# Output projection of a decode attention kernel: weights loaded last, behind the last V tile, and the product in four column tiles

## The chip, the cores and the metric

The kernel runs on one core of one Trainium2 chip. The metric is the device time of one execution in microseconds (us), the median of several. A program on one core has no second die to compare with, so a run is called "slow" only when it is over 1.5% above the fastest run of the same kernel. Profiles show a span a little shorter than the time (1277.4 us for 1279.2 us), and all positions in time below are us from the start of the profiled span.

## The reference, cut to what matters

```python
# A: attention for one new token, batch 2, 16 query heads over 8 KV heads, 32768 cached keys, head size 256
q = (x @ wq) ...                                         # x: [2, 1, 448]
k = jnp.repeat(k_cache, 2, axis=1)                       # k_cache, v_cache: [2, 8, 32768, 256] bf16
v = jnp.repeat(v_cache, 2, axis=1)
p = softmax(einsum("bhqd,bhkd->bhqk", q, k) * Dh ** -0.5)
a = einsum("bhqk,bhkd->bhqd", p, v) ... @ wo             # wo: [4096, 448]
# B: a small dense layer with GELU, w1 [448, 1792], w2 [1792, 448]
g = sigmoid((x * gate_w).sum(-1))
out = g * a + (1 - g) * b                                # [2, 1, 448]
```

The two caches are 537 MB of the 547 MB that the kernel reads, and each byte is read once.

## The kernel before

There are 16 groups (batch, KV head) of 2 K tiles and 2 V tiles. A tile is 8.39 MB: 128 partitions of 64 KB. Three slots hold the tiles; the sync engine (SP) issues the loads in a fixed order and waits before each for the release of its slot. The vector engine transposes each K tile in place, the tensor engine forms scores, then softmax, then the sum weighted over V. I call the last V tiles V29, V30, V31, and the last K tile K31. The tensor engine's main part is a hardware loop; the programs of the other engines are written out in full.

```python
order = [("WQ", 0), ("W12", 0)]
for i in range(NTILES + LAG):                 # LAG = 2
    if i < NTILES: order.append(("K", i))
    if i >= LAG and i - LAG < LASTV: order.append(("V", i - LAG))
order += [("WO", 0), ("V", LASTV)]            # WO takes the slot of V29, V31 the slot of K31
# ... [cut]
PIECES = (64, 32, 16, 8, 8)                   # V31 comes in 5 loads
```

The sync engine works this list in order, so V31, although its own slot (K31's) is free long before, stands behind WO, which waits for V29's weighted sum.

The last group has a form of its own: V is the stationary operand, 256 pairs of weight load and a 2-column matmul for each tile. All other groups have P as stationary operand (24 columns), 64 matmuls of 512 columns in four column tiles; their partial sums are gathered on the vector engine by 8 masked adds, and folded by 2 small matmuls (called OT here).

```python
for r in range(R):                            # last group only
    if r in ends: E.wait(f"pV{ends[r]}", ("piece", ends[r]))
    # ... [cut]
    for j in range(2):
        matmul(ps_o[:, 2*j:2*j+2], kv[:, r, j:Dh:2], pt[:, r16, i, 2*w:2*w+2], ...)

def FIN(c0, c1, key):                         # output product: 32 chunks of 128 rows of WO
    for c in range(c0, c1):
        matmul(ps_a, attnT[:, kvh, j, hh, :], wo_v[:, h, j*Dm:(j+1)*Dm], start=(c == 0), stop=(c == NCH-1))
        # ps_a is 2 partitions x 448

# end of the tensor engine's program
PV(LASTV - 1)
E.wait_total("d_wo")
E.wait("dve", ("O", NG - 2)); E.wait("dve", "bp")
FIN(0, NCH - 4, "FINA")
PV(LASTV)
E.wait("dve", ("O", NG - 1))                  # attnT of the last group
FIN(NCH - 4, NCH, "FIN")
# vector engine: out_sb = ps_a * g + bpart    (2 x 448, called mix here)
# sync engine:   out <- out_sb                (one store)
```

Of the kernel before, what the change touches and what calls it, by code (L numbers as in the profile page):

```python
# [121 lines left out]
def bass_gated_mix__gqa_block_cached__dense_activation_gelu__decode_kernel(  # L122
# [32 lines left out]
    P = 128  # L155
# [22 lines left out]
    GS = NG - 1  # L178
    PIECES = (64, 32, 16, 8, 8)
# [10 lines left out]
    for nm in ("d_w12", "d_wo", "d_x", "d_gw", "d_b", "d_out"):  # L190
        sch.stream(nm, 16)

    with contextlib.ExitStack() as es:
# [12 lines left out]
        b2_bf = PT[0:Bn, 512:512 + Dm]  # L206
        gp_sb = sb("gp_sb", [Bn, Dm], dt.float32)
        b2o, bpart = gp_sb, gp_sb
# [4 lines left out]
        g_sb = sb("g_sb", [Bn, 1], dt.float32)  # L213
        omg = sb("omg", [Bn, 1], dt.float32)
# [6 lines left out]
        out_sb = pexp[0:Bn, 0:Dm]  # L221
# [20 lines left out]
        ps_b = ps_f[0:Bn, 0:Dm]  # L242
        ps_a = ps_f[0:Bn, 0:Dm]
# [21 lines left out]
        order += [("WO", 0), ("V", LASTV)]  # L265
# [71 lines left out]
        def prog_sp(E):  # L337
# [3 lines left out]
            for d in order:  # L341
                for pd in before_of[d]:
                    E.wait("pe", released(pd))
                kind, idx = d
                if kind == "WQ":
                    parts = [(wq_f, A_wq[0:KC * P, :].rearrange("(p k) n -> p (k n)", p=P), "d_wq0"),
                             (wq_r, A_wq[KC * P:Dm, :].rearrange("p (h n) -> (p h) n", h=2), "d_wq1")]
                    for i, (o, src, _) in enumerate(parts):
                        dma(lambda e, o=o, src=src: e.dma_start(o, src), "slot0", ("wq", i))
                elif kind == "W12":  # L350
                    parts = [(w1_f, B_w1[0:KC * P, :].rearrange("(p k) n -> p (k n)", p=P)),
                             (w1_r, B_w1[KC * P:Dm, :].rearrange("p (h n) -> (p h) n", h=2)),
                             (w2_f, B_w2.rearrange("(p f) n -> p (f n)", p=P))]
                    for i, (o, src) in enumerate(parts):
                        dma(lambda e, o=o, src=src: e.dma_start(o, src), "d_w12", ("w12", i))
                elif kind == "WO":
                    dma(lambda e: e.dma_start(wo_v, A_wo.rearrange("(h i j) n -> i h (j n)", i=P, j=2)), "d_wo", "wo")
                elif d == ("V", LASTV):
                    src, base, r0 = kv_src(A_v_cache, idx), slot_of[d] * SLOT, 0
                    for i, n in enumerate(PIECES):  # L360
                        c0, c1 = r0 * Dh, (r0 + n) * Dh
                        dma(lambda e, c0=c0, c1=c1: e.dma_start(ring[:, base + c0:base + c1], src[:, c0:c1]),
                            f"pV{i}", ("piece", i))
                        r0 += n
                else:
                    src = kv_src(A_k_cache if kind == "K" else A_v_cache, idx)
                    dma(lambda e, src=src, d=d: e.dma_start(cut(slot_of[d], 0, SLOT), src),
                        f"slot{slot_of[d]}", ("fill", d))
            E.wait("dve", "mix")
            dma(lambda e: e.dma_start(out[:, 0, :], out_sb), "d_out", "out")  # L370
            E.wait_total("d_out")

        def prog_pe(E):
# [34 lines left out]
            def do_HT():  # L408
                E.wait_total("d_w12")
                for fc in range(FC):  # L410
# [10 lines left out]
            def do_FB():  # L421
                E.wait("dve", "hT")
                for fc in range(FC):
                    E.ins(lambda e, fc=fc: e.matmul(ps_b, hT_bf[:, fc, :], w2_v[:, fc, :],
                                                  start=(fc == 0), stop=(fc == FC - 1)),
                          key=("FB" if fc == FC - 1 else None))
# [52 lines left out]
            def PV(v):  # L479
# [8 lines left out]
                if g < GS:  # L488
                    for r4 in range(0, CR, 4):
                        for w in range(4):  # L490
                            for j in range(4):
# [7 lines left out]
                                if w == 0:  # L499
# [5 lines left out]
                                E.ins(fn, key=(("PV", v) if (r4 == CR - 4 and w == 3 and j == 3) else None))  # L505
                    return
                ends = {}
                if v == LASTV:
                    r0 = 0
                    for i, n in enumerate(PIECES):  # L510
                        ends[r0] = i
                        r0 += n
                for r in range(R):
                    if r in ends:
                        E.wait(f"pV{ends[r]}", ("piece", ends[r]))
                    k, r16 = divmod(t * R + r, CR)
                    w, i = divmod(k, 2)
                    for j in range(2):
                        E.ins(lambda e, kv=kv, r=r, r16=r16, i=i, w=w, j=j, t=t: e.matmul(  # L519
                            ps_o[:, 2 * j:2 * j + 2], kv[:, r, j:Dh:2], pt[:, r16, i, 2 * w:2 * w + 2],  # L520
                            start=(t == 0 and r == 0 and j == 0), stop=(t == NT - 1 and r == R - 1),
                            skip_group_check=True),
                            key=(("PV", v) if (r == R - 1 and j == 1) else None))

            def FIN(c0, c1, key):
                for c in range(c0, c1):
                    h, j = c // 2, c % 2
                    kvh, hh = h // 2, h % 2
                    E.ins(lambda e, c=c, kvh=kvh, hh=hh, j=j, h=h: e.matmul(
                        ps_a, attnT[:, kvh, j, hh, :], wo_v[:, h, j * Dm:(j + 1) * Dm], start=(c == 0), stop=(c == NCH - 1)),  # L530
                        key=(key if c == c1 - 1 else None))

            do_QT()
            do_HT()
# [21 lines left out]
            E.wait_total("d_wo")  # L556
            E.wait("dve", ("O", NG - 2))
            E.wait("dve", "bp")
            FIN(0, NCH - 4, "FINA")
            PV(LASTV)  # L560
            E.wait("dve", ("O", NG - 1))
            FIN(NCH - 4, NCH, "FIN")

        def prog_act(E):
# [8 lines left out]
            for b in range(Bn):  # L573
                dma(lambda e, b=b: e.dma_start(b2_bf[b:b + 1, :], B_b2.rearrange("(o k) -> o k", o=1)), "d_b", ("b2", b))
# [3 lines left out]
            E.ins(lambda e: e.activation(omg[:, :], gs_sb[:, :], ACTF.Exp, scale=-1.0), key="ge")  # L578
# [32 lines left out]
            for g in range(NG):  # L611
                chain(g)
                if g + 1 < NG:
                    fill_A(g + 1)

        def prog_dve(E):
            E.ins(lambda e: e.memset(ps_o[:, :], 0.0), key="o0")
            E.wait("pool", "idf")
# [18 lines left out]
            E.ins(lambda e: e.tensor_scalar(gs_sb[:, :], omg[:, :], 1.0, None, op0=ALU.add), key="g1")  # L637
            E.wait("dve", "g1")
            E.ins(lambda e: e.reciprocal(g_sb[:, :], gs_sb[:, :]), key="g")
            E.wait("dve", "g")  # L640
            E.ins(lambda e: e.tensor_scalar(omg[:, :], g_sb[:, :], -1.0, 1.0, op0=ALU.mult, op1=ALU.add), key="omg")
            E.wait_total("d_b")
            E.wait("dve", "omg")
            E.ins(lambda e: e.tensor_scalar(b2o[:, :], b2_bf, omg[:, 0:1], None, op0=ALU.mult), key="b2o")
# [21 lines left out]
            def do_bp():  # L666
                E.wait("pe", "FB")
                E.wait("dve", "b2o")
                E.ins(lambda e: e.scalar_tensor_tensor(out=bpart[:, :], in0=ps_b, scalar=omg[:, 0:1], in1=b2o[:, :],
                                                       op0=ALU.mult, op1=ALU.add), key="bp")  # L670
# [26 lines left out]
            def do_end(g):  # L697
                b, kvh = grp(g)
                E.wait("pe", ("PV", g * NT + NT - 1))
                col = C_OT  # L700
                src = ps_m
                if g < GS:
                    if g >= 1:
                        E.wait("pe", ("OT", g - 1))
                    for c in range(8):
                        i, w = c // 4, c % 4
                        p = ps_o[:, 512 * w + 256 * i:512 * w + 256 * i + 256]
                        if c == 0:
                            E.wait("dve", "mask")
                            E.ins(lambda e, p=p: e.tensor_scalar(o_sb[:, :], p, mask[:, 0:1], None, op0=ALU.mult),  # L710
                                  key=("OS0", g))
                        else:
                            E.wait("dve", ("OS" + str(c - 1), g))
                            E.ins(lambda e, p=p, c=c: e.scalar_tensor_tensor(  # L714
                                out=o_sb[:, :], in0=p, scalar=mask[:, c:c + 1], in1=o_sb[:, :],
                                op0=ALU.mult, op1=ALU.add), key=(("OS" if c == 7 else "OS" + str(c)), g))
                    E.wait("pe", ("OT", g))
                else:
                    src, col = ps_o, 0
                E.wait("dve", ("RL", g))  # L720
                for j in range(2):
                    E.ins(lambda e, j=j: e.tensor_tensor(attnT[:, kvh, j, :, b], src[:, col + 2 * j:col + 2 * j + 2],  # L722
                                                         rl[g % 2][:, :], ALU.mult),
                          key=(("O", g) if j == 1 else ("O0", g)))
# [13 lines left out]
            E.ins(lambda e: e.scalar_tensor_tensor(out=out_sb, in0=ps_a, scalar=g_sb[:, 0:1], in1=bpart[:, :],  # L738
# [49 lines left out]
```

## Time and profile before

| | before |
|---|---|
| time, median (range) | 1279.25 us (1279.17 to 1279.28) |
| span of the profiled run | 1277.4 us |
| bytes read, mean rate | 547.43 MB, 429 GB/s |
| busy share PE, DVE | 57%, 54% |
| last landing of a load | 1272.19 us |
| from there to the end of the span | 5.2 us |

First some lines of the profile page of the kernel before: its span; in 40 equal slices of the span the busy share of the DMA engines in tenths, and what they moved in GB/s; and of the table of DMA queues (packets, MB, share of 16 engines) the two queues that fetch instructions.

```profile
span 1277.4 us, 8610 instructions
...
DMA  9999999999999999999999999999999999999997
GB/s 410 429 428 443 434 429 429 434 438 433 431 431 437 433 435 429 435 435 433 435 429 437 431 433 437 429 437 431 433 435 429 439 431 433 433 433 437 431 406 304
...
q8 instruction: 11, 0.18, 0.1%
q14 instruction: 7, 0.06, 0.0%
```

The DMA engines are busy from the first slice to the last but one. Only the start and the end of the span can be improved while the bytes stay the same.

The chain of waits of the kernel before, its end in order of time (start, duration, what):

```profile
1245.13 27.06 DMA ring<-in_A_v_cache_dram
...
1272.23 0.60 PE ps_o L519 x16
...
1272.86 0.24 DVE attnT L722 x2
...
1273.14 1.66 PE ps_f L529 x4
...
1274.83 0.67 DVE pexp L738
```

This is the tail: after the last landing (1272.19) come the last 16 small matmuls of the V sum, the scaling into attnT, four output matmuls of 448 columns, and the mix. The store of the result takes the rest, until 1277.4.

The issues on the sync engine's queue, from the timeline of the kernel before (start, duration, what, count):

```profile
1236.11 0.38 SPq L357 DMA_DIRECT2D ring<-in_A_wo_dram  x1
1236.53 10.49 SPq L362 DMA_DIRECT2D ring<-in_A_v_cache_dram  x5
1275.53 0.33 SPq L370 DMA_DIRECT2D out_dram<-pexp  x1
```

WO and V31 were both issued only at 1236, when V29's sum had ended. The view by stretches shows what the DMA did then. Its columns: stretch and its length, then busy time and instruction count of PE, PE weight loads, DVE, ACT, POOL, the granted TensorE clock (the share of full speed that was granted), the DMA share (mean busy share of the 16 DMA engines) and GB/s.

```profile
1236.00:1246.00 10.00, 4.65 (x147) 4.58 (x144) 5.23 (x11) 0.00 (x0) 0.00 (x0) 0.63 0.91 340
1246.00:1262.00 16.00, 10.27 (x151) 5.83 (x147) 0.00 (x0) 0.00 (x0) 0.00 (x0) 0.70 1.03 426
1262.00:1268.00 6.00, 4.19 (x145) 4.02 (x145) 0.00 (x0) 0.00 (x0) 0.00 (x0) 0.53 0.95 393
1268.00:1270.00 2.00, 1.41 (x52) 1.41 (x53) 0.00 (x0) 0.00 (x0) 0.00 (x0) 0.50 0.37 143
1270.00:1272.00 2.00, 1.44 (x49) 1.28 (x45) 0.00 (x0) 0.00 (x0) 0.00 (x0) 0.50 0.08 31
```

The rate dips to 340 GB/s over 1236 to 1246: a hole worth roughly 2 us at the full rate. And the stream does not end at once: in 1268 to 1270 only 0.37 and in 1270 to 1272 only 0.08 of the 16 DMA engines' time is busy. A share of 0.06 is one engine of sixteen.

Each load of a tile or of WO is served in 16 parts (it leaves 16 landing records), and the trace records when each part's completion arrives. These landing records are not a view of the profile; here they are counted from the start of the run's own span. For the earliest and the latest of the 16 they give (I call the difference the lag):

```
kernel before      earliest   latest    latest minus earliest
first K tile          38.33     40.69     2.36
tile at 638          638.24    640.58     2.34
tile at 696          696.31    699.24     2.92
tile at 948          947.92    951.80     3.87
K31                 1199.52   1203.36     3.84
V30                 1238.22   1242.20     3.98
WO                  1248.03   1252.64     4.61
V31, last piece     1267.73   1272.19     4.45
```

From tile to tile both columns advance by 19.35 us, except where the lag steps up.

### The profile page before, as it was taken

Reading aid. Unit: us, or ns where it says so; the run is one execution under the profiler, and the core shown is the slowest. Engines: PE = TensorE matmul, PEld = TensorE weight load, DVE = VectorE, ACT = ScalarE, POOL = GpSimd, SP = SyncE. Lnnn points to the kernel's source line nnn. Section 1 sums busy time; section 2 is a strip of 40 time slices with the busy share of each in tenths; the row PEclk is TensorE's granted clock in tenths of the full one; section 3 lists DMA queues with packets and bytes.
Section 4 is the critical chain, followed back from the end, with each engine's and each line's share of the span. In section 5 each row is a group of like instructions: output and inputs, shape, how many; then the busy total and the mean of one; then the engine's idle time right before and its main releaser. Section 6 shows DMA issues by size and latency. Waiting matters only on the chain.

```text
span 1277.4 us, 8610 instructions
## 1 busy us (share of the span) xinstructions
PE 733.8 (57%) x4917; PEld 176.8 (14%) x2453; DVE 685.6 (54%) x528; ACT 42.4 (3%) x182; POOL 2.5 (0%) x11
## 2 busy tenths in 40 slices
PE   3666665645576453765645666455764546656466
PEld 3111111101011010111101111010110101111024
DVE  1676546745357563556735467453565536567340
ACT  1000000000000000000000000000000000000000
POOL 0000000000000000000000000000000000000000
PEclk9778787867877777887677778678777678877776
DMA  9999999999999999999999999999999999999997
GB/s 410 429 428 443 434 429 429 434 438 433 431 431 437 433 435 429 435 435 433 435 429 437 431 433 437 429 437 431 433 435 429 439 431 433 433 433 437 431 406 304
DMA packets 12754, 547.68 MB, mean 429 GB/s; under 512 B 1336, under 2 KB 3520, under 8 KB 3904
## 3 DMA queue, kind: packets, MB, share of 16 engines
q1 hardware_dynamic: 12580, 547.43, 99.3%
q8 instruction: 11, 0.18, 0.1%
q14 instruction: 7, 0.06, 0.0%
q10 hardware_dynamic: 156, 0.01, 0.0%
HBM read 547.43 MB, written 0.00 MB: 429 GB/s over the span
## 4 chain that ended last, share of the span: by engine, by line
DMA 58%; DVE 23%; PE 16%; ACT 2%; issue 1%; SPq 0%; another core or an unknown queue 0%; ACTq 0%
DMA ring<-in_A_k_cache_dram 55%; DVE ring L675 20%; PE ps_o L319 5%; PE ps_s L446 4%; PE ps_s L319 4%; DMA ring<-in_A_v_cache_dram 2%; PE ps_o L500 2%; DVE mx L679 1%; ACT pexp L604 1%; PE ps_m L468 1%; PE ps_m L463 0%; PE ps_m L458 0%; DVE gmax L681 0%; DVE ls L690 0%; DVE o_sb L714 0%
## 5 line engine op out<-in xcount | busy, mean ns | idle before, releaser
L675 DVE STREAM_TRANSPOSE ring<-ring 128x2048 uint32<-128x2048 uint32 x256 | 565.1, 2274 | 315.9 <-DMA ring<-in_A_k_cache_dram 315.9
L446 PE MATMUL ps_s<-ring,Abd 128*128 128x512 bf16 x1024 | 426.7, 417 | 370.7 <-DVE ring L675 370.1
L319 PE MATMUL ps_s<-ring,Abd 128*128 128x512 bf16 x1024 | 422.8, 413 | 0.0
L446 PEld LDWEIGHTS ps_s<-ring,Abd 128*128 128x128 bf16 x1024 | 106.1, 104 | 782.5 <-DVE ring L675 415.5
L319 PE MATMUL ps_o<-ring,PT 128*24 128x512 bf16 x1440 | 122.2, 454 | 0.0
L695 DVE STREAM_TRANSPOSE PT<-pexp 128x1024 bf16<-128x1024 bf16 x16 | 19.9, 1244 | 81.7 <-PE ps_o L319 81.7
L475 PE MATMUL ps_m<-sel,o_sb 128*128 128x2 f32 x60 | 15.2, 358 | 80.2 <-DVE o_sb L714 80.2
L500 PE MATMUL ps_o<-ring,PT 128*24 128x512 bf16 x480 | 56.8, 463 | 0.0
L714 DVE SCALAR_TENSOR_TENSOR o_sb<-ps_o,mask,o_sb 128x256 f32<-128x256 f32 x105 | 50.8, 484 | 3.7
L679 DVE TENSOR_REDUCE mx<-ps_s 128x1 f32<-128x1024 f32 x16 | 19.6, 1224 | 59.7 <-PE ps_s L319 59.7
L600 ACT ACTIVATE negm<-ps_m 128x1 f32<-128x1 f32 x16 | 2.7, 171 | 1159.9 <-PE ps_m L463 1159.9
L500 PEld LDWEIGHTS ps_o<-ring,PT 128*24 128x24 bf16 x480 | 14.0, 107 | 99.6 <-issue 99.3
L475 PEld LDWEIGHTS ps_m<-sel,o_sb 128*128 128x128 f32 x60 | 13.9, 320 | 98.9 <-DVE o_sb L714 98.9
L468 PE MATMUL ps_m<-ls,ones_f 128*128 128x2 f32 x32 | 8.8, 345 | 28.2 <-DVE ls L690 28.2
L690 DVE TENSOR_SCALAR ls<-par,lsum 128x2 f32<-128x2 f32 x16 | 3.7, 229 | 31.0 <-ACT pexp L604 31.0
L458 PE MATMUL ps_m<-ident_f,mx 128*1 128x128 f32 x32 | 6.1, 270 | 23.6 <-DVE mx L679 23.6
L595 ACT COPY Abd<-qrep 32x16 bf16<-32x16 bf16 x128 | 19.4, 198 | 0.6
L519 PE MATMUL ps_o<-PT,ring 128*128 128x2 bf16 x512 | 14.7, 165 | 7.5 <-DMA ring<-in_A_v_cache_dram 4.9
L604 ACT ACTIVATE pexp<-ps_s,negm 128x1024 bf16<-128x1024 f32 x16 | 17.8, 1114 | 0.5
L722 DVE TENSOR_TENSOR attnT<-ps_o,rl 128x2 bf16<-128x2 f32 x2 | 0.2, 156 | 30.2 <-PE ps_o L519 30.2
L519 PEld LDWEIGHTS ps_o<-PT,ring 128*128 128x128 bf16 x512 | 14.2, 104 | 8.4 <-DMA ring<-in_A_v_cache_dram 5.7
L722 DVE TENSOR_TENSOR attnT<-ps_m,rl 128x2 bf16<-128x2 f32 x30 | 3.4, 158 | 16.6 <-PE ps_m L475 16.6
(63 smaller groups left out, 94.9 us busy)
## 6 DMA issues: line engine op xcount, KB each, us to landing
ring<-in_A_v_cache_dram SPq DMA_DIRECT2D x1, 4096.0 KB, 25.8
ring<-in_A_wo_dram SPq DMA_DIRECT2D x1, 3584.0 KB, 16.5
ring<-in_A_wq_dram SPq DMA_DIRECT2D x1, 3072.0 KB, 10.5
ring<-in_A_v_cache_dram SPq DMA_DIRECT2D x1, 2048.0 KB, 23.9
ring<-in_B_w_dram SPq DMA_DIRECT2D x1, 1568.0 KB, 18.5
ring<-in_B_w_dram SPq DMA_DIRECT2D x1, 1344.0 KB, 13.7
ring<-in_A_v_cache_dram SPq DMA_DIRECT2D x1, 1024.0 KB, 25.7
ring<-in_A_v_cache_dram SPq DMA_DIRECT2D x2, 512.0 KB, 26.7
```

The costliest lines, as they stand in the source:

```text
L319: return e.add_instruction(mybir.InstMatmult(name=f"I-{nc.next_id()}", engine=mybir.EngineType.PE, ldweights=False, ins=[e.lower_ap(x), e. ...
L446: fn = lambda e, o=o, x=x, st=st, sp=sp, s=s, w=w: e.matmul(o, a_win(s, w), x, start=st, stop=sp, skip_group_check=True)
L468: E.ins(lambda e: e.matmul(ps_m[:, C_L:C_L + 2], ones_f[:, :], ls2[:, :], start=True, stop=True), key=("L", g))
L475: E.ins(lambda e, j=j: e.matmul(ps_m[:, C_OT + 2 * j:C_OT + 2 * j + 2], o_sb[:, j:Dh:2], sel[:, :], start=True, stop=True), key=(("OT", g) ...
L500: fn = lambda e, o=o, x=x, wt=wt, st=st, sp=sp, j=j: e.matmul(o, wt, x, start=st, stop=sp, skip_group_check=True)
L519: E.ins(lambda e, kv=kv, r=r, r16=r16, i=i, w=w, j=j, t=t: e.matmul(ps_o[:, 2 * j:2 * j + 2], kv[:, r, j:Dh:2], pt[:, r16, i, 2 * w:2 * w ...
L595: E.ins(lambda e, o=o, Q=Q, c=c: e.copy(o[:, :, c:c + 2], qrep[32 * Q:32 * Q + 32, :, kvh, :, b]), key=(("A", g) if (Q == 3 and c == 16) e ...
L604: E.ins(lambda e: e.activation(pexp[:, :].rearrange("p (r i a) -> p i r a", r=CR, i=2), ps_s[:, :].rearrange("p (i r a) -> p i r a", i=2, ...
L675: E.ins(lambda e: e.transpose(k_words(idx, blk), k_words(idx, blk)), key=("T", idx, blk))
L679: E.ins(lambda e: e.tensor_reduce(mx[:, :], ps_s[:, :], AX.X, ALU.max), key=("MX", g))
L695: E.ins(lambda e: e.transpose(PT[:, :], pexp[:, :]), key=("PT", g))
L714: E.ins(lambda e, p=p, c=c: e.scalar_tensor_tensor(out=o_sb[:, :], in0=p, scalar=mask[:, c:c + 1], in1=o_sb[:, :], op0=ALU.mult, op1=ALU.a ...
```

## The change

The intent: V31 no longer waits behind WO, and what remains to be done after the last byte becomes small. Per output chunk, four matmuls of 112 columns in four column tiles of the tensor engine's array replace one of 448; the result then lies in 8 rows (2 at each of the partitions 0, 32, 64, 96) of 112. The diff, cut to its core:

```diff
-    GS = NG - 1
-    PIECES = (64, 32, 16, 8, 8)
+    PIECES = (64, 32, 32)
+    WOP = (0, 8, 14, 16)
+    DQ = Dm // 4
...
-        order += [("WO", 0), ("V", LASTV)]
+        order += [("V", LASTV), ("WO", 0)]
...
                 elif kind == "WO":
-                    dma(lambda e: e.dma_start(wo_v, A_wo.rearrange("(h i j) n -> i h (j n)", i=P, j=2)), "d_wo", "wo")
+                    src = A_wo.rearrange("(h i j) n -> i h (j n)", i=P, j=2)
+                    for i, (h0, h1) in enumerate(zip(WOP, WOP[1:])):
+                        dma(lambda e, src=src, h0=h0, h1=h1: e.dma_start(wo_v[:, h0:h1, :], src[:, h0:h1, :]),
+                            f"pW{i}", ("wo", i))
...
-            dma(lambda e: e.dma_start(out[:, 0, :], out_sb), "d_out", "out")
+            dma(lambda e: e.dma_start(out[0, 0, :].rearrange("(j n) -> j n", j=4), out_sb[0:P:32, :]), "d_out", "out0")
...   (the scalar engine, at its end)
+            dma(lambda e: e.dma_start(out[1, 0, :].rearrange("(j n) -> j n", j=4), out_sb[1:P:32, :]), "d_out", "out1")
...   (PV: the last group loses its own form; its V31 is taken piece by piece in the form of the others)
+                for pc, ws in parts:
+                    if pc is not None:
+                        E.wait(f"pV{pc}", ("piece", pc))
...
+                    for q in range(4):
+                        E.ins(lambda e, ...: e.matmul(
+                            ps_a[32 * q:32 * q + Bn, :], attnT[:, kvh, j, hh, :],
+                            wo_v[:, h, j * Dm + q * DQ:j * Dm + (q + 1) * DQ],
+                            start=(c == 0), stop=(c == NCH - 1), skip_group_check=True), ...)
...   (end of the tensor engine's program)
             PV(LASTV - 1)
-            E.wait_total("d_wo")
+            PV(LASTV)
             E.wait("dve", ("O", NG - 2))
             E.wait("dve", "bp")
-            FIN(0, NCH - 4, "FINA")
-            PV(LASTV)
+            FIN(0)
+            OT(NG - 1)
+            FIN(1)
             E.wait("dve", ("O", NG - 1))
-            FIN(NCH - 4, NCH, "FIN")
+            FIN(2)
...   (not shown: gate broadcast to the 8 rows by 4 tiny matmuls, bias and layer B in the same layout, masked adds in the order of the pieces)
```

## The prediction

> **What bounds the kernel now.** DMA. The page counts 547.68 MB at 429 GB/s over a span of 1277.4 us, and the DMA row is at 9 tenths in every slice but the last. In the trace's landing records each 8.39 MB tile follows the one before by 19.35 us (433 GB/s), for the earliest and for the latest of its 16 parts alike; the latest lags 2.4 us at first, 3.8 to 4.6 at the end. [...] only the end has anything to give.
>
> **The end before.** Timeline: the weighted sum of V29 ends at 1236.1, and only then are WO and, behind it, V31 issued. V30's 16 parts land from 1238.2 to 1242.2. By stretches the DMA dips: 340 GB/s over 1236 to 1246. But that is early parts running dry: the latest part has V30 until 1242.2, WO until 1252.6, V31 until 1272.2, without a hole. The chain of waits ends on it, so the filled dip gives little. After it come the last 16 matmuls 0.60, attnT 0.24, four output matmuls 1.66 (cold clock, 0.37 each), mix 0.67, output store about 1.9; with gaps 5.2 us.
>
> **What changes.**
> 1. V31 is issued when K31's slot is free, about 1224.8 instead of 1236.5, behind V30. Latest part: 1242.2 + 19.4 = 1261.6.
> 2. WO comes last. Its 1792-byte packets run at some 13.3 per us and engine (79 ns each): estimate 9.6 us for the 128 of one engine; on the latest part it took 10.4. Last landing estimate 1271.8, against 1272.2: 0.4 us gained, uncertain by 0.8. Bytes are unchanged.
> 3. V31's sum takes the 24-column form (64 matmuls in 6.2 us cold for a tile). Its end, the masked adds (0.5 us each, 4 left), OT (1.0) and attnT (0.24) finish around 1266, or 1270 behind FIN(0): hidden under WO.
> 4. After the last WO piece: 16 matmuls of 112 columns in 4 column tiles. [...] the trace agrees (64 matmuls of 512 in 6.2 us, a quarter of 0.427 each). Estimate 0.56 us instead of 1.66.
> 5. mix 128x112 instead of 2x448: 0.34 instead of 0.67, from the slope between 256 columns (0.48) and 448 (0.67).
> 6. Early work added (gate broadcast, 56 short matmuls instead of 14, split bias): the first K tile lands at 40.7, the old work ended at 35.4, so it is hidden. The second store adds at most 0.1.
>
> **On the critical path.** 0.60, 0.24 and gaps of 0.1 leave it, 1.1 and 0.3 come off FIN and mix, 0.4 off DMA: about 2.5 us.
>
> **Predicted: 1276.7 us**, 8 in 10 between 1275.2 and 1278.2. Faster by over 2%: 0.01; within: 0.98; slower: 0.01.
>
> **What would show it.** Last WO landing at 1271.0 to 1272.6; no DMA dip at 1236 to 1246; tile cadence 19.35 unchanged; about 3 us from last landing to the end; last attnT done before the last WO piece.
>
> **What would make it wrong.** Column tiles not overlapping when each matmul reloads weights (FIN(1) 4.5 us, FIN(2) 1.5: slower by 2 to 4); PE waiting for instructions (a 1.9 us idle marked issue at 1247); an instruction fetch delaying the latest DMA part (its lag stepped by 0.6 and 1.0 us at 696 and 950); WO's packets slower when all engines run them.

The sum: 0.60 + 0.24 + 0.1 + 1.1 + 0.3 + 0.4 = 2.74 us, less 0.1 for the second store, put at about 2.5, hence 1276.7. That only the end has anything to give stands on the DMA row, 9 tenths in every slice but the last. That column tiles run side by side is shown by the measurement in point 4, in the trace of the kernel before: 64 matmuls of 512 columns in column tiles took 6.2 us from 1229.88, 0.097 us each, where without column tiles they followed each other every 0.427 us (from 1208.35 to 1210.91, granted clock 0.50). The 0.56 us is an estimate; from the last four output matmuls of the kernel before (0.37 us from one to the next, 1.66 in all) I get much the same: a quarter of 1.48, and the 0.18 that is left over, 0.55. "Cold" means a granted clock of about 0.5 (0.50 for the output matmuls, 0.58 over the 6.2 us). That the tensor engine's idle 1.9 us at 1247 was a wait for instructions is not shown; a fetch of 16384 bytes on q8 started at 1246.53.

## The result

| | before | after |
|---|---|---|
| time, median (range), 4 runs each | 1279.26 us (1279.17 to 1279.36) | 1277.61 us (1277.52 to 1278.06) |
| span of the profiled run | 1277.4 | 1276.2 |
| last landing | 1272.19 | 1272.49 |
| last landing to end of mix | 3.31 | 1.06 |
| end of mix to end of span | 1.92 | 2.68 |

The ratio is 0.9988 with a 95% interval of 0.997 to 1.0005. A ratio is the mean time of one kernel's fast runs over that of the other's of the same rounds, so it is not quite the ratio of the medians in the table. The ranges of the two kernels do not touch: the gain of 1.65 us, 0.13%, is small but seen in each run. The profiled run of the changed kernel was its slowest (1278.06), so its span shows only 1.2 us of the gain.

The lines of the changed kernel that answer to those above, first from its page:

```profile
span 1276.2 us, 8103 instructions
...
DMA  9999999999999999999999999999999999999997
GB/s 410 428 432 434 438 431 428 438 430 438 433 427 436 433 438 433 429 435 433 434 431 435 431 438 429 435 433 429 442 428 435 435 427 436 435 433 435 427 429 300
...
q8 instruction: 9, 0.15, 0.0%
q14 instruction: 7, 0.06, 0.0%
```

Then the end of its chain of waits:

```profile
1236.12 35.28 DMA ring<-in_A_wo_dram
...
1271.44 1.75 PE ps_f L537 x58
...
1273.22 0.33 DVE pexp L764
```

The small matmuls of the V sum and the scaling have left the tail. What remains is one block of output matmuls and a mix of half the length. The block starts at 1271.44, just after the landing of WO's second piece (1271.40); the third landed at 1272.49 while the block ran.

The timeline of the changed kernel at the end: the issues on the sync engine's queue (SPq) and on the scalar engine's (ACTq), and the last work of PE and DVE, with the idle time before it and what ended it in brackets.

```profile
1225.45 1.28 SPq L368 DMA_DIRECT2D ring<-in_A_v_cache_dram  x3
...
1235.69 27.67 SPq L362 DMA_DIRECT2D ring<-in_A_wo_dram  x3
...
1268.14 1.66 PE L537 MATMUL ps_f<-ring,attnT 128*2 128x112 bf16 x64 [3.01 <-DMA ring<-in_A_wo_dram]
...
1269.73 1.01 PE L492 MATMUL ps_m<-sel,o_sb 128*128 128x2 f32 x4
1270.79 0.23 DVE L748 TENSOR_TENSOR attnT<-ps_m,rl 128x2 bf16<-128x2 f32 x2 [4.59 <-PE ps_m L492]
...
1271.44 1.73 PE L537 MATMUL ps_f<-ring,attnT 128*2 128x112 bf16 x64 [0.69 <-DMA ring<-in_A_wo_dram]
1273.22 0.33 DVE L764 SCALAR_TENSOR_TENSOR pexp<-ps_f,g,bpart 128x112 bf16<-128x112 f32 x1 [2.21 <-PE ps_f L537]
1273.58 0.65 SPq L376 DMA_DIRECT2D out_dram<-pexp  x1
1273.59 0.57 ACTq L628 DMA_DIRECT2D out_dram<-pexp  x1
```

V31 is now issued at 1225.45. The 64 output matmuls of pieces two and three take 1.73 us, 27 ns for each matmul of 112 columns, where one of 448 had taken 0.37 us at the same low clock (0.50 granted). Alone, a matmul of 112 columns would take a quarter of 0.37 us, an estimate of 93 ns; so the four column tiles run side by side. The attnT of the last group is ready at 1271.02, before the last piece. And the store now costs 0.65 us of issue instead of 0.33.

The view by stretches of the changed kernel, same columns as before:

```profile
1236.00:1246.00 10.00, 3.28 (x28) 1.18 (x12) 4.92 (x11) 0.00 (x0) 0.00 (x0) 0.73 0.95 406
1246.00:1262.00 16.00, 7.92 (x96) 1.14 (x40) 2.90 (x6) 0.00 (x0) 0.00 (x0) 0.71 0.97 401
1262.00:1268.00 6.00, 1.89 (x16) 0.43 (x16) 0.97 (x2) 0.00 (x0) 0.00 (x0) 0.50 1.01 365
1268.00:1270.00 2.00, 1.86 (x66) 1.70 (x66) 0.00 (x0) 0.00 (x0) 0.00 (x0) 0.50 0.23 86
1270.00:1272.00 2.00, 1.30 (x32) 1.22 (x36) 0.23 (x2) 0.00 (x0) 0.00 (x0) 0.50 0.07 25
```

The hole at 1236 to 1246 is nearly gone: 406 instead of 340 GB/s. Yet the last landing of this run is not earlier but 0.30 us later (in a second profile of the same kernel, after_again, it came at 1271.95, 0.24 us earlier). The stream again thins out at the end, to 0.23 and then 0.07: for the last two to four microseconds about one DMA engine works alone. The landing records say the same:

```
kernel after       earliest   latest    latest minus earliest
tile at 638          638.46    641.82     3.37
tile at 948          948.06    952.44     4.39
V29                 1218.99   1223.38     4.39
V30                 1238.34   1243.69     5.35
V31, last piece     1257.95   1263.20     5.25
WO, third piece     1267.58   1272.49     4.91
```

All 16 parts but one had landed 3.3 us before the last (the second latest part of WO's third piece landed at 1269.18).

### The profile page after: what moved, and what is told of

It is laid out like the page before. It is cut to its first block, busy times and chain, and to the rows that moved or that the text cites. A ratio compares the mean times of both kernels' runs of the same rounds, so it can differ in the third digit from the quotient of the medians.

```text
span 1276.2 us, 8103 instructions
## 1 busy us (share of the span) xinstructions
PE 725.7 (57%) x4683; PEld 165.2 (13%) x2155; DVE 690.8 (54%) x545; ACT 42.4 (3%) x182; POOL 2.5 (0%) x11
## 3 DMA queue, kind: packets, MB, share of 16 engines
q1 hardware_dynamic: 12328, 547.43, 99.4%
HBM read 547.43 MB, written 0.00 MB: 429 GB/s over the span
## 4 chain that ended last, share of the span: by engine, by line
DMA 58%; DVE 21%; PE 18%; ACT 2%; issue 1%; SPq 0%; another core or an unknown queue 0%
DMA ring<-in_A_k_cache_dram 56%; DVE ring L700 18%; PE ps_s L463 5%; PE ps_s L322 5%; PE ps_o L322 5%; DMA ring<-in_A_wo_dram 3%; PE ps_o L523 2%; DVE mx L704 1%; ACT pexp L616 1%; PE ps_m L485 1%; PE ps_m L480 1%; PE ps_m L475 0%; DVE gmax L706 0%; DVE ls L715 0%; DVE gmx L710 0%
## 5 line engine op out<-in xcount | busy, mean ns | idle before, releaser
L700 DVE STREAM_TRANSPOSE ring<-ring 128x2048 uint32<-128x2048 uint32 x256 | 565.1, 2275 | 319.2 <-DMA ring<-in_A_k_cache_dram 319.2
L322 PE MATMUL ps_o<-ring,PT 128*24 128x512 bf16 x1504 | 128.4, 454 | 0.0
L523 PE MATMUL ps_o<-ring,PT 128*24 128x512 bf16 x544 | 64.8, 476 | 11.1 <-DMA ring<-in_A_v_cache_dram 11.1
L742 DVE SCALAR_TENSOR_TENSOR o_sb<-ps_o,mask,o_sb 128x256 f32<-128x256 f32 x112 | 54.1, 483 | 9.6 <-PE ps_o L523 5.7
L607 ACT COPY Abd<-qrep 32x16 bf16<-32x16 bf16 x128 | 19.4, 198 | 0.6
L739 DVE TENSOR_SCALAR o_sb<-ps_o,mask 128x256 f32<-128x256 f32 x16 | 7.1, 446 | 14.2 <-PE ps_o L322 14.2
L480 PE MATMUL ps_m<-ones_f,gmx 1*128 1x1 f32 x32 | 6.6, 271 | 9.9 <-DVE gmx L710 9.9
L485 PEld LDWEIGHTS ps_m<-ls,ones_f 128*128 128x128 f32 x32 | 6.8, 265 | 29.6 <-DVE ls L715 29.6
```

Of the source, the lines that this page charges most:

```text
L322: return e.add_instruction(mybir.InstMatmult(name=f"I-{nc.next_id()}", engine=mybir.EngineType.PE, ldweights=False, ins=[e.lower_ap(x), e. ...
L480: E.ins(lambda e: e.matmul(ps_m[:, C_BC:C_BC + 1], gmx[:, :], ones_f[0:1, 0:1], start=True, stop=True), key=("M2", g))
L485: E.ins(lambda e: e.matmul(ps_m[:, C_L:C_L + 2], ones_f[:, :], ls2[:, :], start=True, stop=True), key=("L", g))
L523: fn = lambda e, o=o, x=x, wt=wt, st=st, sp=sp, j=j: e.matmul(o, wt, x, start=st, stop=sp, skip_group_check=True)
L607: E.ins(lambda e, o=o, Q=Q, c=c: e.copy(o[:, :, c:c + 2], qrep[32 * Q:32 * Q + 32, :, kvh, :, b]), key=(("A", g) if (Q == 3 and c == 16) e ...
L700: E.ins(lambda e: e.transpose(k_words(idx, blk), k_words(idx, blk)), key=("T", idx, blk))
```

## The experiments

Two questions. First, where does the gain come from: theory A, as predicted, only from a shorter chain behind the last landing; rival B, from the filled hole in the DMA stream. Second, what is the late part, which holds up the end of both kernels: theory C, one DMA engine that also fetches the vector engine's instructions and is put back by each fetch; rival D, something else, with which the fetches only coincide. Theory C comes from these times of the changed kernel, from the trace's packets of q14 and the landing records. The last column comes from all 16 landing records: with the landings of a tile sorted and counted from the earliest, it is the one place that moves between the tile before the fetch and the tile after it.

```
fetch on q14 at    next step of the lag     the place that moves
86.89              none                     0.51 to 1.47
385.39             +0.5  (at  389.3)        1.41 to 2.36
625.87             +1.0  (at  641.8)        2.39 to 3.37
934.07             +1.0  (at  952.4)        3.41 to 4.39
1239.83            +1.0  (at 1243.7)        4.39 to 5.35
301.90             none                     0.18 to 0.82
1078.93            none                     0.78 to 1.38
```

The five fetches of the first rows move one place, each time by 0.95 to 0.98 us, and each time from where the one before had left it; the other fifteen stay where they were within some hundredths. The first of them stays hidden because other parts were later still. The two fetches of the last rows move another place, which is never the latest.

Runs of one call share a chip and the runs of the kernel before; different calls had different chips, so each is given with its difference from the kernel before of the same call (means of fast runs).

### e1_hold_v: V31 held back again

```diff
+                if d == ("V", LASTV):
+                    E.wait("pe", ("PV", LASTV - 2))
```

> The changed kernel, but the last V tile is held back until V29's weighted sum is done (about 1236), as before the change; WO still last. Theory A (only the chain behind the last landing became shorter; the early issue of V31 fills a hole that the latest DMA part never had): 1277.6 us within 0.5, last WO landing at 1272.5 within 0.4, while the DMA share dips again at 1238 to 1242. Rival B (the gain is the filled hole in the DMA stream, some 2 us of full rate between 1236 and 1246): 1279 to 1280 us, last landing later by 1.5 to 2.3.

Measured: 1277.24 us (1277.19 to 1277.35), 1.96 below the kernel before; the changed kernel itself was 1.56 below in its runs and 1.80 in a later call. Last landing 1272.07, just outside the 1272.5 within 0.4 that I expected. So the early issue of V31 is worth nothing, as theory A has it. But one expectation of mine failed: the dip did not come back, the rate over 1236 to 1246 was 407 GB/s:

```profile
1236.00:1246.00 10.00, 3.73 (x32) 1.18 (x12) 4.49 (x11) 0.00 (x0) 0.00 (x0) 0.73 0.95 407
```

So the hole is not made by the late issue; it is there when WO is first in line. In the kernel before, the trace counts 51 packets of WO in the microsecond 1238 to 1239, then 142, 197, 209: a slow start, in part because the parts of V30 end one after the other between 1238.2 and 1242.2. Another part is no hole at all: in the changed kernel over 1264 to 1267, where WO alone moves and the engines have no gap (DMA share 1.06), its packets of 1792 bytes make 381 GB/s, while the tiles' packets of 65536 bytes make 433. What the rest is no run here shows. For the hole itself the five kernels of this question decide:

```
kernel             GB/s 1236 to 1246   last landing
before                  340              1272.19
e7_columns_alone        342              1272.15
after                   406              1272.49
e1_hold_v               407              1272.07
e2_order_alone          414              1271.99
```

With the hole filled the last landing came between 0.20 us earlier and 0.30 later than before the change (after_again: 0.24 earlier), not some 2 us earlier. The latest part was never dry: it had V30 to do until 1242. Rival B is out.

### e2_order_alone: the order without the column tiles

On the kernel before:

```diff
-        order += [("WO", 0), ("V", LASTV)]
+        order += [("V", LASTV), ("WO", 0)]
...   (WO in 3 loads, as in the change)
             PV(LASTV - 1)
-            E.wait_total("d_wo")
+            PV(LASTV)
             E.wait("dve", ("O", NG - 2))
             E.wait("dve", "bp")
-            FIN(0, NCH - 4, "FINA")
-            PV(LASTV)
+            E.wait("pW0", ("wo", 0))
+            FIN(0, 16, "FINA")
+            E.wait("pW1", ("wo", 1))
+            FIN(16, 28, "FINB")
+            E.wait("pW2", ("wo", 2))
             E.wait("dve", ("O", NG - 1))
-            FIN(NCH - 4, NCH, "FIN")
+            FIN(28, NCH, "FIN")
```

> The kernel before with the order alone changed: V31 first in its 5 pieces and old form, WO last in 3 pieces, output product still one tile of 448 columns, 32 matmuls. Theory A: order alone is a loss, because the 32 output matmuls (0.37 us each cold) now queue behind WO: 16 of them from WO's first piece at about 1268, so the last ends near 1280 and the time is 1282 to 1285 us. Rival B (order is what gains, column tiles a detail): below 1279.2 us.

Measured: 1280.15 us (1279.88 to 1281.35), 1.16 above the kernel before. The direction is right, the size is not: I expected 1282 to 1285. The timeline of this run, two lines:

```profile
1267.73 8.24 PE L535 MATMUL ps_f<-ring,attnT 128*2 128x448 bf16 x32 [4.17 <-DMA ring<-in_A_wo_dram]
...
1276.01 0.67 DVE L747 SCALAR_TENSOR_TENSOR pexp<-ps_f,g_sb,gp_sb 2x448 bf16<-2x448 f32 x1 [12.19 <-PE ps_f L535]
```

The 32 matmuls took 8.24 us, not 12, because the granted clock rose to full speed on the way (the last column but two):

```profile
1270.00:1272.00 2.00, 2.00 (x7) 0.69 (x6) 0.00 (x0) 0.00 (x0) 0.00 (x0) 0.53 0.06 24
1272.00:1274.00 2.00, 2.00 (x12) 0.92 (x11) 0.00 (x0) 0.00 (x0) 0.00 (x0) 1.00 0.00 0
```

Still, with 448 columns per matmul the product ends 4.0 us after the last landing (1271.99): the order alone turns a wait for DMA into a wait for PE.

### e7_columns_alone: the column tiles without the order

The changed kernel with WO ahead of V31, V31 in 5 pieces and the last group's old form:

```diff
-        order += [("V", LASTV), ("WO", 0)]
+        order += [("WO", 0), ("V", LASTV)]
-    PIECES = (64, 32, 32)
-    WOP = (0, 8, 14, 16)
+    PIECES = (64, 32, 16, 8, 8)
+    WOP = (0, 16)
...   (last group's form and end of the tensor engine's program as before, FIN in column tiles)
```

> The kernel before with column tiles alone: output product, gate and bias as in the change, but WO still ahead of V31, V31 in 5 pieces and its old form. Last landing as before, 1272.2; then 0.60 + 0.24 + 0.1 of the old chain, FIN 0.45, mix 0.33, stores 2.65: 4.4 us instead of 5.2, so 1278.4 within 0.4, about half of the gain. If the gain is mainly the order's: 1279.0 or more.

Measured: 1278.83 us (1278.63 to 1279.01), 0.44 below the kernel before, just outside what I gave (1278.0 to 1278.8). The end of its chain of waits:

```profile
1272.19 0.60 PE ps_o L537 x16
...
1272.81 0.24 DVE attnT L757 x2
...
1273.10 0.57 PE ps_f L548 x16
...
1273.69 0.33 DVE pexp L773
```

The four times four column-tile matmuls take 0.57 us where four of 448 columns took 1.66, and the mix 0.33 instead of 0.67. From the last landing (1272.15) to the end of mix it is 1.88 us instead of 3.31; but from there to the end of the span 2.68 instead of 1.92. So neither half carries the change: columns alone give about 0.4 us, order alone loses 1.2, both together give 1.6 to 1.8.

### e3_probe: whether one DMA engine is late

Between V31 and WO stand 15 tiny loads; load n fills 32 bytes in each of n partitions.

```diff
+                    for n in range(1, 16):
+                        dma(lambda e, n=n: e.dma_start(probe[0:n, 16 * n:16 * n + 16], A_wo[0:n, 0:16]),
+                            f"pr{n}", ("pr", n))
```

> The changed kernel plus 15 probe loads between V31 and WO: probe n loads 32 bytes into each of partitions 0 to n-1. [...] If the lag is not one engine's, all probes look alike. Time within 1.5 us of the changed kernel.

Foretold for a lag that is one engine's: from some n on, each probe has one landing at about 1263, some 5 us after its others at about 1258. The landing records of this one look (1278.62 us, correct), of which a probe of n partitions has n:

```
n    landings
3    1258.31 1258.53 1259.25
4    1258.49 1258.72 1259.42 1262.74
5    1258.67 1258.90 1258.90 1259.60 1262.92
7    1259.01 1259.26 1259.27 1259.73 1259.77 1259.95 1263.28
14   thirteen from 1259.38 to 1261.26, one at 1264.65
```

From four partitions on, each probe has exactly one late landing, by 3.3 to 3.4 us (I had expected some 5). So the probes are not all alike, and one part is late in each, not several. That fits one DMA engine that is late, as does the DMA share of 0.07 at the end of the changed kernel. Which of the sixteen it is, is not shown.

### e4_more_instr: more instructions on the vector engine

```diff
                 if blk == 0:
+                    for n in range(8):
+                        E.ins(lambda e, n=n: e.memset(pad[:, 8 * idx + n:8 * idx + n + 1], 0.0))
                     wait_fill(E, ("K", idx))
```

> The changed kernel with 256 more one-element memsets on the vector engine, 8 before each K tile, while it waits for the DMA. Theory C (each fetch of vector-engine instructions, queue 14, 8 KB, goes through one and the same DMA engine and puts it back by about 1 us for good; the last landing is this engine's): 2 more such fetches, the latest part lags 7 instead of 5 us at the end, and the time goes up by 1.5 to 2.5 us, to 1279.1 to 1280.1. Rival D (the lag has another cause, the coincidence in time is chance): time unchanged within 0.3 us, lag 5.

Measured: 1279.52 us (1279.49 to 1279.70), 0.34 above the kernel before, so 1.9 to 2.1 above the changed kernel. Instruction fetches in its page:

```profile
q14 instruction: 9, 0.07, 0.0%
```

Nine instead of seven: two more for 256 instructions, so an estimated 128 instructions of 64 bytes in each fetch of 8192. The lag at the end is 6.33 us instead of 4.9, the last landing comes at 1273.91. The vector engine had waited for the DMA where the memsets stand (in the changed kernel its 319.2 us of idle time before the K transposes ended on the loads), and the loads are the same 547.43 MB. Theory C stands.

### e5_pair_transposes: fewer instructions, same work

```diff
-            return cut(slot_of[("K", idx)], lo, CR * Dh).bitcast(dt.uint32)
+            return cut(slot_of[("K", idx)], lo, 2 * CR * Dh).bitcast(dt.uint32)
...
-                E.ins(lambda e: e.transpose(k_words(idx, blk), k_words(idx, blk)), key=("T", idx, blk))
+                if blk % 2 == 0:
+                    E.ins(lambda e: e.transpose(k_words(idx, blk), k_words(idx, blk)), key=("T", idx, blk + 1))
```

> The changed kernel with the K transposes of the vector engine joined in pairs (128 instructions of 4096 words instead of 256 of 2048): same work, 128 instructions fewer on that engine. Theory C (each vector-engine instruction fetch puts the late DMA engine back by 1 us): one fetch fewer, lag 4 instead of 5, time 1276.2 to 1277.0. Rival D (lag has another cause): 1277.6 within 0.3.

Measured: 1276.74 us (1276.64 to 1276.84), 2.52 below the kernel before.

```profile
q14 instruction: 6, 0.05, 0.0%
```

Six fetches instead of seven, lag 3.71, last landing 1271.24.

### e8_dve_loop: the vector engine's main part as a loop

```diff
-            for kind, idx in order:
-                ...
+            for i in range(LAG):
+                K(i)
+            E.loop((NTILES - LAG) // UNIT, steps, ("dve", ("PT", 0)))
+            do_end(NG - 1)
...   (scalar engine: one small copy per group puts the group's result in its place, since a loop writes to a fixed one)
+                    E.wait("dve", ("O", g - 1))
+                    E.ins(lambda e, ...: e.copy(attnT[:, kvh, :, :, b], oT[:, (g - 1) % 3, :, :]), key=("CP", g - 1))
```

> The changed kernel with the vector engine's main part written as a hardware loop (5 turns of 6 K tiles), as the tensor engine's already is; a copy per group on the scalar engine puts the group's result in its place. Theory C: instruction fetches of the vector engine in the main part fall from 5 to 1 or 2, the late DMA engine lags about 2 us like the others, the last landing comes at about 1269.7 and the time falls to 1274.2 to 1275.8. Rival D: the lag stays near 5 and the time within 0.5 of 1277.6.

Measured: median 1275.65 us, 3.60 below the kernel before. The four runs fall in two pairs, 1274.84 and 1274.93, 1276.38 and 1276.50, of which the slower pair lies above the 1275.8 that I gave as the upper end; the profile is of the first run. Why there are two pairs is open, no profile of the slower pair was taken.

```profile
q14 instruction: 4, 0.03, 0.0%
```

Four fetches, of which two are the vector engine's. The lag at the end is 1.79 us and the second latest part is 0.03 us before the latest: the late engine is now level with others. The last landing comes at 1269.28.

Put together, from the profiled runs (a fetch on q14 is counted as the vector engine's if it is not one of the two, near 302 and near 1000 to 1080, that every one of these kernels has):

```
kernel                 fetches of DVE   lag at last landing   last landing   time (median)
before                      5                 4.45              1272.19        1279.26
after                       5                 4.91              1272.49        1277.61
after_again                 5                 4.24              1271.95        1277.56
e4_more_instr               7                 6.33              1273.91        1279.52
e5_pair_transposes          4                 3.71              1271.24        1276.74
e8_dve_loop                 2                 1.79              1269.28        1275.65
```

About 1 us for each fetch, down to the point where other parts are as late. Rows with the same number of fetches still differ by up to 0.7 us in lag, because the place that the fetches move does not start level: before its first fetch it was 0.51 us behind the earliest in the changed kernel, 0.00 in after_again.

The landing records of all thirteen traces bear theory C out. Of the vector engine's fetches, 53 stand alone between two tiles, and each of these moves just one of the sixteen places, by 0.92 to 1.02 us, and leaves the others within some hundredths. The lone fetches on q14 near 302 and near 1000 to 1080 move one place by 0.57 to 0.66, and of the 65 lone fetches of 16384 bytes on q8 all but one move one place by 1.5 to 1.7. So it is not the number of instructions in itself that costs time, but each fetch, and what decides the end is that all of the vector engine's fetches fall on the same place. The packets of the trace do not name their DMA engine: that this place is the engine that e3 found late is inferred (in e3's trace too it is the latest place from 625 on). It is not known why a fetch of 8192 bytes, 0.3 us long in the trace, puts that engine back by three times as much.

### e6_store_one_queue and e9_store_adjacent: the dearer store

The prediction gave the second store 0.1 us; the time from the end of mix to the end of the span grew by 0.76. First, both stores from the sync engine:

```diff
             dma(... out_sb[0:P:32, :]), "d_out", "out0")
+            dma(... out_sb[1:P:32, :]), "d_out", "out1")     # and none from the scalar engine
```

> The changed kernel with both output stores issued from the sync engine, one after the other. In the changed kernel the two issues, at the same moment from two engines, take 0.65 and 0.57 us, while the one issue of before took 0.33. If the two engines' issues get in each other's way: each takes about 0.33 here, time within 0.15 of the changed kernel. If a store from rows 32 partitions apart is slow by itself: two times 0.6, time up by 0.5 to 0.7. If the second queue is what is slow: time down by 0.3 to 0.6.

Measured: 1277.75 us (1277.60 to 1277.87), 1.52 below the kernel before. The two issues in its timeline:

```profile
1273.17 0.66 SPq L376 DMA_DIRECT2D out_dram<-pexp  x1
1273.87 0.51 SPq L377 DMA_DIRECT2D out_dram<-pexp  x1
```

This fits none of my three cases whole. The first store is alone in its time and still takes 0.66 us, so two engines issuing at once is not the cause; yet the time hardly moved, since the end of mix to the end of the span was 2.66 us, as with two engines. Then a kernel with a wrong result, whose stores read 4 adjacent partitions instead of 4 that lie 32 apart:

```diff
-  out_sb[0:P:32, :]   ...   out_sb[1:P:32, :]
+  out_sb[0:4, :]      ...   out_sb[4:8, :]
```

> Wrong result on purpose: the changed kernel, its two stores taken from 4 adjacent partitions each instead of 4 partitions 32 apart. In the changed kernel the first packet of a store leaves 1.3 to 1.5 us after the issue starts, before the change 0.74. If the step of 32 partitions is what costs: issue back to 0.33, first packet after about 0.75. If it is the four rows of 224 bytes: issue 0.6 and first packet after 1.3, as in the changed kernel.

```profile
1273.34 0.35 SPq L376 DMA_DIRECT2D out_dram<-pexp  x1
1273.35 0.29 ACTq L628 DMA_DIRECT2D out_dram<-pexp  x1
```

The issues are back to 0.35 and 0.29 us, the first packets leave 0.79 and 0.77 us after the start of the issue (1.49 and 1.22 us in the changed kernel, 0.75 before), as the first case has it, and from the end of mix to the end of the span it is 2.13 us instead of 2.68. So 0.55 of the 0.76 us go with the step of 32 partitions; the remaining 0.2 us belong to the four rows of 224 bytes and the second store together. As it is one look of a kernel with a wrong result, its time (1277.24) is no more than a hint.

### e10_loop_pairs_cuts and after_again: a version that beats both

The loop of e8, the paired transposes of e5, and WO cut finer, because in the changed kernel PE needed 1.75 us from the landing of WO's second piece while the third landed after 1.09:

```diff
-    WOP = (0, 8, 14, 16)
+    WOP = (0, 8, 13, 15, 16)
...
             FIN(2)
+            FIN(3)
```

> A version meant to beat both: the changed kernel with the vector engine's loop, its transposes joined in pairs, and WO in 4 pieces cut at heads 8, 13, 15 instead of 3 cut at 8, 14, so that less output product is left behind the last pieces. Theory: last landing about 1269.2 as with the loop alone, the output product ends 0.4 to 0.6 after it instead of 0.8, so 0.3 us off the loop version: 1274.5 in its faster executions, median 1274.3 to 1276.0. If nothing is to be had from the cut: 1274.9 to 1276.5 as the loop alone.

> The changed kernel once more, on the same chip as the version above, for a direct comparison: 1277.6 within 0.4, the version above 2 to 3 us faster.

Measured on one chip, 5 runs each: this version 1274.35 us (1274.24 to 1274.92), the changed kernel 1277.56 (1277.48 to 1277.68), the kernel before 1279.34 (1279.14 to 1279.68, 9 runs). Its ratio to the kernel before is 0.9962 (0.9949 to 0.9976). It is correct. The end of its chain of waits:

```profile
1267.79 1.10 PE ps_f L538 x38
...
1269.00 0.84 PE ps_f L538 x24
...
1269.87 0.33 DVE pexp L784
```

The last landing is at 1269.41; the product ends 0.40 us later (0.68 in the changed kernel and in e8). Against e8's profiled run the span is 0.51 us shorter: the last landing is 0.13 later, the chain to the end of mix 0.28 shorter, and the end of mix to the end of the span 0.36 shorter. The last of these is not the cuts' doing: it lies between the store's landing and the end of the span, and e1, with the store of the changed kernel, has the same (2.39 us against 2.68). What the pairs and the cuts each add to the loop was not separated. The gain on the changed kernel, 3.1 us by the means, is a little more than the 2 to 3 that I expected. The second pair of times that the loop alone had did not show in these five runs.

## Why the prediction was right

The time, 1277.61 us, lies in the range (1275.2 to 1278.2) and the gain of 1.65 us is two thirds of the 2.5 foretold. Point by point:

- *DMA bounds the kernel, only the end has anything to give.* Held. The cadence of 19.35 us per tile is the same in all kernels, 433 GB/s.
- *The filled dip gives little.* Held, by e1, e2 and e7 against the changed kernel. That the dip came from the late issue, as I had it, was wrong: with WO behind V31 it stays away even when V31 is late.
- *Last landing 0.4 us earlier, uncertain by 0.8.* It was 0.30 later in the profiled run, which was the slowest, and 0.24 earlier in after_again; both lie inside the stated 0.8, so the sum held only within a band twice as wide as the gain. What was off in the profiled run is "Latest part: 1242.2 + 19.4 = 1261.6": V31's last piece landed at 1263.20, because V30's latest part came at 1243.69 instead of 1242.20; its lag was 4.39 instead of 3.84 before V30, and the instruction fetch at 1239.83 added 0.96, where the kernel before has its fetch only at 1245.04, after V30. The prediction had named this risk without costing it. WO's own 9.29 us on the latest part was near the 9.6 of the estimate.
- *The chain behind the last landing: 0.60 and 0.24 leave it, 1.1 and 0.3 come off.* Held: from the last landing to the end of mix 1.06 us instead of 3.31, so 2.25 against 2.34 foretold with gaps. The last attnT was ready at 1271.02, not at about 1270, but still 0.4 before WO's second piece. The column tiles do run side by side although each matmul loads its weights anew (64 weight loads for the 64 matmuls from 1271.44 on): 27 ns each for 112 columns, and 0.57 us for sixteen in e7 (0.56 foretold).
- *mix 0.34.* Measured 0.33.
- *The second store adds at most 0.1.* This term was mis-sized: 0.76 us. e9, one look, puts 0.55 of it on the step of 32 partitions in the source of the store.
- *Early work is hidden.* Held: the first K tile's and all later landings keep their cadence.

In sum, for the two profiled runs: +0.30 (last landing) - 2.25 (chain) + 0.76 (store) = -1.19 us, which is the difference of the spans, 1277.42 and 1276.23. The other runs of the changed kernel have spans of 1275.7 to 1275.8, so they gained about 0.4 us more; after_again's profile shows where: -0.24 - 2.25 + 0.75, about -1.73 us. So the gain is the chain's, and the dearer store took a third of it back.

## What to carry to other kernels

In a kernel that streams at the full rate, look at when the last of the 16 parts of a load lands, not at the mean rate: here one part, 4.9 us behind the earliest in the changed kernel, decided the end, and a hole in the stream that this part did not have was free (340 against 406 GB/s over 1236 to 1246, last landing 1272.19 against 1272.49). Put last what needs the least work after it has landed, and make that work short in the same step; either half alone gave little or lost. And count instructions: here the vector engine's program, written out in full, was fetched by DMA 8192 bytes at a time, 5 times (2 as a loop), and each fetch put the late part back by 0.92 to 1.02 us. A loop or fewer, larger instructions can be worth more than the tuning of the tail: by the means, 1.8 to 2.0 us for the loop alone (e8) and 3.1 us for e10's loop, pairs and finer cuts together, against 1.6 to 1.8 for the change.
